# A transformer block on one core: output products of attention at a stretch, and row loads, normalization, row maxima and differences at other places

## The chip, the cores and the metric

The kernel runs on one core of a Trainium2 chip. The metric is the time of one execution on the device, in microseconds (us). The engines are TensorE (PE, with its weight loads as PEld), VectorE (DVE), ScalarE (ACT), GpSimd (POOL), and SyncE (SP), which here only issues DMAs. Each engine carries out its own list of instructions in the order of the program, and waits where one of them needs something from another engine or from a DMA.

## The reference

The input is 2048 rows of 512 numbers. The block is an attention with a memory between four segments of 512 rows, and a feed-forward part; all numbers are fp32.

```
mod = silu(c) @ w_mod                       # six rows: sa, ca, ga, sb, cb, gb
h = layernorm(x) * (1 + ca) + sa
x = x + ga * attention(h)                   # 32 heads of 16
h = layernorm(x) * (1 + cb) + sb
x = x + gb * (gelu(h @ w1 + b1) @ w2 + b2)  # 1792 inner columns

# attention, for each of four segments s of 512 rows and each head
p = softmax(qs @ ks.T / 4 + causal mask)
o = g * (phi(qs) @ M) / (phi(qs) @ z) + (1 - g) * (p @ vs)
M = M + phi(ks).T @ vs;  z = z + sum(phi(ks))
# then o @ wo
```

## The kernel before

There are three stages: projections (until about 190 us), attention (about 190 to 475 us), and the feed-forward part. Between the last two lies what this text calls the joint.

**Attention** takes the heads four at a time within a segment: 32 such groups, Q = 0 to 31, each of two pairs of heads, P = 2Q and 2Q + 1. For each pair, scores are made twice. `s_part` makes them with queries on the partitions, for the row maxima (L606, maxima on DVE at L613); parts 0 to 3 are query blocks with 512, 384, 256 and 128 keys. `st_part` makes them transposed, with the maxima already subtracted through three more rows of `qst` (L693); ACT takes the exponential (L708, L719) and POOL sets what lies above the diagonal to zero (L696, `causal`). `pv_part` multiplies with the values (L733). Both kinds of scores take the six PSUM banks `att` in turn.

For a pair of heads the smaller score blocks (256 and 128 keys) share a bank. For these there are two ways to the maxima: a third product adds the mask (L645) and one reduction on DVE takes both maxima (L617), or each head has a masked maximum of its own (L613). `PRM["m"]` and `PRM["mq"]` choose.

The maxima of a group go back into `qst` in three steps: `m_rows` splits them on POOL (L661), `m_put` turns them on PE (L667) with a copy on ACT, and `m_send` is a small DMA into `qst` (L675), issued by SP for the first groups and by ACT for the later ones (`PRM["msa"]`). Until it has landed, the group's transposed scores can't begin.

**The order** is written out by hand. One loop (L1013) runs over Q; this text calls one pass "loop Q". Its string `ORDER` names the score parts (S and T, with the part's number; the first mention in a pass is for pair 2Q, the second for 2Q + 1; S runs four pairs ahead) and twenty slots c0 to c19 between them:

```
ORDER = ('S1 c0 T2 T3 T2 c1 S2 c2 S3 T3 S3 c3 c4 c5 T5 S0 c6 c7 T0 c8 c9 '
         'T1 T4 S2 c10 c11 T5 S1 c12 T4 S0 c13 T0 c14 T1 c15 c16 c17 c18 c19')
```

Everything else has a position, 20 times the loop plus the slot; `ap(position, f, ...)` puts it there. So 466 is slot c6 of loop 23. Some positions that do not change: `m_rows` of group Q at 20Q - 26, `m_put` at 20Q - 17 (slot c3 of loop Q - 1), `load_stacks` (two DMAs of 384 KB) at c15, `pv_part` at c11 and c16 to c18.

**Two groups make a unit U.** The sums go to memory and come back packed (`pv_store`, `pv_in`); the reciprocals of the denominators are stored and spread (`den`, `den_store`, `rb_in`); `mix` joins them with the memory's part; `o_hi` and `o_lo` split the result for three products. For segments 0 to 2, `wo_part` multiplies with `wo` (L821, three products of 512 columns in the bank `mm`): for each of four row blocks four parts, at positions 240 + 160s + `PRM["wo"][s]`, then `wo_out` adds the input rows (DVE at L839, POOL at L837) and `wo_store` writes the rows to memory. These are then read back by `ln2_load` (positions `in`), their statistics are taken (`stat`, `rstd`), and `ln2_apply` normalizes them (`on`; L568, on POOL for segment 0 and on DVE for segment 1). `ln2_turn` transposes them on PE (L574; positions `ht` 502, 509, 516, 523 for segment 0).

**The joint** begins at L1161: what is left of the last units, the third segment's output products (`wo_seg`, `wo_late`), and the first operands of the feed-forward part, which uses a scheme with seven products for each 2 x 2 blocks. `r_sub` makes differences of operands on DVE (L886), `r_hi` and `r_lo` split them.

**The feed-forward part** runs over quads n = 0 to 13 (L1113), each with steps 0 to 6; `bg(n, i, f, ...)` puts background work at step i of quad n, where i over 6 runs on into the next quad. The rows of segments 2 and 3 are loaded, normalized and turned there.

## Time and profile before

| | us |
|---|---|
| three executions | 785.7, 789.17, 786.71 |
| median | 786.71 |
| the profiled execution | 789.61 |
| its span | 787.9 |

The span is that of the engines' instructions within the profiled execution. Busy times and waits below come from this one execution. In the views, a row of the timeline or the chain begins with the start and the length in us, then the engine, the line of the kernel and what is written and read; "x3" is the number of instructions merged into the row; brackets tell how long the engine stood idle before it and what ended that. A row of the waits tells who waited, for whom, the total in us, how often, and the longest. A row of stretches gives for each engine the busy time with the number of instructions, then the granted clock of TensorE, the busy share of the DMA engines and GB/s. Ends of matmuls are modelled: matmuls overlap, and the start of the next one tells more than the end.

### The profile page before, as it was taken

How to read it: one execution, taken by the hardware profiler on the slowest of the kernel's cores; microseconds unless marked ns; L12 is line 12 of the kernel's file. 1: busy time of each engine (PE TensorE's matmuls, PEld its weight loads, DVE VectorE, ACT ScalarE, POOL GpSimd, SP SyncE). 2: the span in 40 equal slices, each digit the busy share in tenths (PEclk: the TensorE clock that was granted, in tenths of full speed). 3: DMA queues.
4: the chain of work that ended last, by engine and by line, in shares of the span. 5: the costliest groups of instructions: out<-in, count | busy, mean ns of one | idle time of the engine just before them, and what ended most of it. 6: DMA issues, size and time to landing. Idle time of an engine off the chain costs nothing.

```text
span 787.9 us, 14128 instructions
## 1 busy us (share of the span) xinstructions
PE 767.7 (97%) x4577; PEld 532.6 (68%) x4577; DVE 553.6 (70%) x1456; ACT 472.6 (60%) x910; POOL 315.4 (40%) x535
## 2 busy tenths in 40 slices
PE   8999999999999999998999998999999999999998
PEld 4887776877554445554445446887888888888887
DVE  5686687548988788887977898867669764432423
ACT  3565546474888877776778676666645346652221
POOL 1357367261568556655696661133000404200000
PEclk9999999999999999999999999999999999999999
DMA  9596857497465566768677854595565624445543
GB/s 337 183 313 230 296 179 231 147 297 244 130 199 158 165 203 194 214 197 231 189 178 205 238 155 146 186 311 189 194 235 195 204 96 161 161 148 172 171 127 116
DMA packets 108818, 156.10 MB, mean 198 GB/s; under 512 B 16324, under 2 KB 55620, under 8 KB 108744
## 3 DMA queue, kind: packets, MB, share of 16 engines
q1 hardware_dynamic: 106758, 153.36, 62.1%
q10 hardware_dynamic: 1986, 1.84, 0.7%
q8 instruction: 36, 0.59, 0.3%
q14 instruction: 38, 0.31, 0.1%
HBM read 93.95 MB, written 60.83 MB: 196 GB/s over the span
## 4 chain that ended last, share of the span: by engine, by line
PE 74%; DMA 7%; DVE 7%; POOL 5%; issue 3%; ACT 3%; ACTq 0%; SPq 0%; DVEq 0%; POOLq 0%
PE att L693 7%; PE pv L733 7%; PE bx L1080 7%; PE att L606 6%; PE q L313 6%; PE bx L1346 5%; PE by L1346 5%; PE bv L1346 5%; PE k L313 4%; PE bv L1080 3%; PE v L464 3%; PE spare L1346 2%; PE mm L821 2%; DMA qst<-ms 2%; PE mm L1346 2%
## 5 line engine op out<-in xcount | busy, mean ns | idle before, releaser
L613 DVE CUSTOM_DVE_ANT_0 dump<-att,maskb 128x384 bf16<-128x384 f32 (+3 forms) x400 | 188.3, 524 | 38.8 <-PE att L606 22.1
L708 ACT ACTIVATE pt<-att 128x384 f32<-128x384 f32 (+1 forms) x256 | 125.5, 545 | 17.1 <-PE att L693 13.1
L696 POOL TENSOR_SCALAR_AFFINE_SELECT pt<-pt 128x256 f32<-128x256 f32 x256 | 104.1, 419 | 72.9 <-ACT pt L708 44.2
L693 PE MATMUL att<-qst,kst 99*128 99x256 bf16 (+3 forms) x512 | 108.0, 301 | 6.0 <-DMA qst<-ms 5.4
L606 PE MATMUL att<-kst,qst 96*128 96x384 bf16 (+3 forms) x400 | 94.0, 317 | 0.3 <-DVE nm L613 0.2
L693 PEld LDWEIGHTS <-kst 99*128 99x128 bf16 x512 | 44.1, 98 | 73.7 <-issue 36.2
L719 ACT ACTIVATE pt<-att 128x256 f32<-128x256 f32 (+1 forms) x128 | 62.3, 494 | 33.0 <-PE att L693 19.8
L865 POOL TENSOR_TENSOR wb<-wa 128x256 f32<-128x256 f32 x24 | 20.3, 845 | 151.8 <-DMA wa<-in_w 149.1
L733 PE MATMUL pv<-pt,V 128*32 128x512 f32 (+1 forms) x992 | 79.8, 439 | 0.0
L136 DVE TENSOR_TENSOR gl<-s,gh 128x512 fp32r<-128x512 f32 x34 | 24.1, 708 | 42.2 <-ACT gh L133 42.2
L733 PEld LDWEIGHTS pv<-pt,V 128*32 128x32 f32 x992 | 25.8, 109 | 35.9 <-issue 30.6
L133 ACT ACTIVATE gh<-s 128x512 fp32r<-128x512 f32 x34 | 21.3, 628 | 46.8 <-PE spare L1346 17.1
L606 PEld LDWEIGHTS <-qst 96*128 96x128 bf16 x400 | 32.9, 99 | 17.7 <-issue 12.4
L1085 ACT ACTIVATE s<-s,b1t 128x512 f32<-128x512 f32 x42 | 30.3, 722 | 21.9 <-DVE s L1089 21.8
L1089 DVE TENSOR_TENSOR s<-bv,s 128x512 f32<-128x512 f32 x28 | 19.3, 690 | 31.4 <-PE bv L1080 21.3
L613 DVE DVE_READ_ACCUMULATOR2_ANT nm<- 128x1 f32 x400 | 33.3, 83 | 0.0
L617 DVE TENSOR_REDUCE nm<-att 128x2 f32<-128x512 f32 (+1 forms) x56 | 28.7, 553 | 3.8 <-PE att L645 3.8
L509 POOL TENSOR_TENSOR q<-qr,q 128x512 bf16<-128x512 f32 x16 | 18.7, 1167 | 26.8 <-ACT q L508 26.5
L500 POOL TENSOR_SCALAR qp<-qp 128x512 f32<-128x512 f32 x12 | 19.2, 1603 | 24.6 <-ACT qp L495 24.6
L136 DVE TENSOR_TENSOR w1ml<-s,w1mh 128x512 fp32r<-128x512 f32 x18 | 13.0, 722 | 21.7 <-ACT w1mh L133 21.7
L661 POOL TENSOR_TENSOR nm<-nm 128x16 f32<-128x16 f32 x64 | 13.9, 218 | 33.7 <-DVE nm L613 31.0
L133 ACT ACTIVATE w1mh<-s 128x512 fp32r<-128x512 f32 x18 | 11.3, 628 | 26.3 <-PE spare L1346 11.6
(362 smaller groups left out, 2090.0 us busy)
## 6 DMA issues: line engine op xcount, KB each, us to landing
GD<-s SPq DMA_DIRECT2D x56, 256.0 KB
s<-GD SPq DMA_DIRECT2D x52, 256.0 KB
kst<-KD SPq DMA_DIRECT2D x32, 384.0 KB
qst<-QD SPq DMA_DIRECT2D x32, 384.0 KB
TD<-ts SPq DMA_DIRECT2D x32, 256.0 KB
xt<-X2D SPq DMA_DIRECT2D x28, 256.0 KB
wa<-in_w SPq DMA_DIRECT2D x28, 256.0 KB
QD<-q SPq DMA_DIRECT2D x16, 384.0 KB
```

Source lines behind the costliest of these rows:

```text
L133: act.activation(hi, src, AF.Copy)
L136: lo_eng.tensor_tensor(out=lo, in0=src, in1=hi.bitcast(F32), op=ALU.subtract)
L313: pe.matmul(ps, a[:, k, 128 * g:128 * g + 128], b[k], start=(k == 0 and i == 0), stop=(k == KB - 1 and i == 2))
L606: pe.matmul(ps, q_of(P, h, i), k_of(P, h, 128 * (i + 1)), start=True, stop=True)
L613: v.tensor_tensor_reduce(out=dump[n_dump[0] % 2][:, :n], in0=src, in1=maskb[:, 512 - n:], scale=-1.0, scalar=-4 * NEG, op0=ALU.add, op1=AL ...
L693: pe.matmul(ps, k[:99, e, 128 * j:128 * j + 128], q[:99, e, 128 * j:512], start=True, stop=True)
L696: pool.affine_select(out=t, in_=t, pattern=pattern, compare_op=ALU.is_ge, fill=0.0, base=0, channel_multiplier=-1)
L708: act.activation(pt[:, h, :], ps[:, :n], AF.Exp, scale=0.25)
L719: act.activation(pt, pv_, AF.Exp, scale=0.25)
L733: pe.matmul(ps[32 * c:32 * c + 32, lo:hi], V[4 * s + j][:, VW * hd:VW * hd + 32], pt[:, c % 2, lo - o:hi - o], start=start, stop=stop)
L1080: pe.matmul(ps, a[:, i, k, :], b[k], start=start and k == 0 and c == 0, stop=k == 1 and c == 2, skip_group_check=not start)
L1346: pe.matmul(ps, a[:, c], w[:, lo:hi], start=(f == 0 and i == 0), stop=(last and i == 2))
```

## The change

- The output products of segments 0 and 1 move from the slots c2 and c5 to c3 and c4, which follow each other without scores between them; in segment 2 the four parts at c2, c5, c8 and c14 move to c3, c3, c4, c4. `wo_x`, `wo_out` and `wo_store` move with them.
- `m_send` comes one slot after `m_put` instead of two, and SP issues it for groups under 13 instead of 10.
- For groups under 14 the blocks of 256 keys take masked maxima instead of a mask product and a reduction.
- The row loads and the normalization of segments 0 and 1 have other positions.
- In the joint, the subtraction `t2` comes ahead of a weight split, and `t3` and `t4` come in quad 0 behind `o_hi` and `o_lo` of unit 14.
- The rows of segment 3 are loaded in four steps instead of one, and the turns of segments 2 and 3 come two steps later.

```diff
- 'msl': 2,
- 'msa': 10,
+ 'msl': 1,
+ 'msa': 13,
...
- 'wo': [[20 * i + o for i in range(8) for o in (2, 5)]] * 2 + [[20 * i + o for i in range(4) for o in (2, 5, 8, 14)]],
+ 'wo': [[20 * i + o for i in range(8) for o in (3, 4)]] * 2 + [[20 * i + o for i in range(4) for o in (3, 3, 4, 4)]],
...
- 'ln': [{'in': [388, 397, 408, 417], 'stat': [418, 425, 437, 445], 'rstd': 449, 'on': [460, 467, 481, 487]},
-        {'in': [528, 537, 548, 568], 'stat': [565, 577, 585, 597], 'rstd': 603, 'on': [624, 626, 628, 630]}],
+ 'ln': [{'in': [327, 367, 387, 407], 'stat': [418, 425, 437, 445], 'rstd': 449, 'on': [455, 475, 479, 495]},
+        {'in': [527, 530, 547, 567], 'stat': [565, 577, 585, 597], 'rstd': 603, 'on': [624, 626, 628, 630]}],
...
- 'm': [1, 1, 1, 1],
+ 'm': [[0, 1, 0, 1], [1, 1, 1, 1]],
...
-                if PRM["m"][2 * p + i] and Q >= PRM["mq"]:
+                if PRM["m"][Q >= PRM["mq"]][2 * p + i]:
...
         r_hi(0, "t1")
+        r_sub(0, "t2")
         w_lo(0, 0)
-        r_sub(0, "t2")
         w_hi(0, 1)
...
         rest(14, "mix")
-        for n in ("t3", "t4"):
-            r_sub(0, n)
...
-        for n, i, f, *a in ((0, 0, rest, 14, "o_hi", "o_lo"), (0, 1, w_hi, 0, 2), (0, 1, w_hi, 0, 3),
+        for n, i, f, *a in ((0, 0, rest, 14, "o_hi", "o_lo"), (0, 0, r_sub, 0, "t3"), (0, 0, r_sub, 0, "t4"), (0, 1, w_hi, 0, 2), (0, 1, w_hi, 0, 3),
...
-        bg(3, 2, ln2_load3)
+        for b, i in enumerate((2, 3, 5, 6)):
+            bg(3, i, ln2_load3, b)
...
-                bg(n, 12 + d, ln2_turn, s, d, (mm, spare)[d % 2])
+                bg(n, 14 + d, ln2_turn, s, d, (mm, spare)[d % 2])
```

More of the change, by code (lines that the diff above doesn't have):

```diff
@@ L1223, in block_kernel, with ln2_load3 @@
             bg(n, i, f, *a)
-        def ln2_load3():
-            ln2_load(3, None, [gx[0](f"x3_{b}", F32) for b in range(4)])
+        x3 = []
+        def ln2_load3(b):
+            if b == 0:
+                x3.extend(gx[0](f"x3_{i}", F32) for i in range(4))
+            ln2_load(3, b, x3)
         def ln2_applies(s, lo, hi):
```

## The prediction

> **What bounds the kernel now.** I read first the page, then who TensorE (PE) waited for, then the chain of work in order of time, then timelines of single stretches.

> ```profile
> span 787.9 us, 14128 instructions
> ...
> PE 767.7 (97%) x4577; PEld 532.6 (68%) x4577; DVE 553.6 (70%) x1456; ACT 472.6 (60%) x910; POOL 315.4 (40%) x535
> ```

> PE is busy 97% of the span, so a change pays only where it shortens PE's own work or one of its few waits. These are the waits that matter (us in total, times, longest):

> ```profile
> PE att L693 <- DMA qst<-ms: 5.4, 5, 2.9
> PE bv L821 <- DVE ol L810: 2.8, 1, 2.8
> PE att L643 <- ACT pt L719: 2.0, 3, 1.1
> ...
> PE pv L667 <- POOL nm L661: 1.6, 2, 1.2
> ...
> PE mm L574 <- DVE xt L568: 0.5, 1, 0.5
> PE mm L574 <- ACT hr L576: 0.4, 1, 0.4
> ```

> The chain of waits gives the loop times; the eight matmuls of `pv` come once a loop:

> ```profile
> 237.00 0.99 PE pv L733 x8
> ...
> 244.70 1.00 PE pv L733 x8
> ...
> 328.59 1.00 PE pv L733 x8
> ...
> 337.14 0.99 PE pv L733 x8
> ...
> 354.24 0.99 PE pv L733 x8
> ...
> 361.15 9.02 DMA qst<-ms
> ...
> 376.04 0.99 PE pv L733 x8
> ```

> An early loop takes 7.70 us, one with output products 8.55, and the two from 354.24 to 376.04 take 21.80, that is 4.70 more than 2 x 8.55. The chain there lies on the send of the maxima of Q=21, which needed 9.02 us. PE idled 2.9 of it; the rest is the clock:

> ```profile
> 360.00:380.00 20.00, 17.07 (x133) 8.43 (x132) 15.59 (x68) 11.83 (x26) 10.08 (x21) 0.91 0.85 230
> ```

> A granted clock of 0.91 over 20 us is 1.8 us lost: 2.9 + 1.8 = 4.7. [...]

> **Sends.** `msl` moves the send one slot, past nothing on its own queue: nothing. `msa` moves Q=10 to 12 from ACT to SP:

> ```profile
> 266.88 1.36 ACTq L675 DMA_DIRECT2D qst<-ms  x1
> ```

> ACT's queue stands still while it issues, and the exponentials behind it hold the banks PE wants: the 2.0 us of L643 above, 3 times, these three. On SP the sends of Q below 10 cost PE nothing visible. But Q=11 is sent just behind the load of `gab`, and may land late: I take -1.5 (between -2.2 and 0).

> **Row maxima.** For Q under 14 the 256-wide pair loses its mask product, and gets two masked maxima for one reduction (28 times).

> ```profile
> 242.04 0.27 PE L645 MATMUL att<-maskb,identb 128*128 128x256 bf16 x1
> 242.16 0.22 PE L643 MATMUL att<-kst,qst 96*128 96x128 bf16 x1
> ...
> 242.27 0.27 PE L645 MATMUL att<-maskb,identb 128*128 128x256 bf16 x1
> 242.56 0.32 PE L693 MATMUL att<-qst,kst 99*128 99x384 bf16 x1
> ```

> ```profile
> L613 DVE CUSTOM_DVE_ANT_0 dump<-att,maskb 128x256 bf16<-128x256 f32 x72 | 27.5, 420 | 3.8 <-ACT pt L708 3.1 <-issue 0.7
> ...
> L617 DVE TENSOR_REDUCE nm<-att 128x2 f32<-128x512 f32 x28 | 19.3, 690 | 2.9 <-PE att L645 2.9
> ```

> A mask product costs PE 0.12 (242.04 to 242.16), so 28 are 3.4 us at most. But L693 at 242.56 started 0.29 after the product ahead of it, which itself takes 0.12: PE was already waiting there for a bank, so of a loop's two removed products the first only lengthens that wait. DVE pays 2 x 27.5/72 - 19.3/28 = 0.07 us each. With one product saved and some 0.05 given back in a loop, twelve loops make -0.8 (between -3.4 and +2).

> **Output products.** Two parts of three products stood at c2 and c5, now at c3 and c4, behind `m_put`. The same place in loop 20:

> ```profile
> 358.24 0.50 PE L606 MATMUL att<-kst,qst 96*128 96x384 bf16 x2
> ...
> 359.20 0.48 PE L821 MATMUL mm<-woh,oh 128*128 128x512 f32 x1
> ...
> 359.99 0.29 PE L606 MATMUL att<-kst,qst 96*128 96x128 bf16 x2
> 360.11 0.33 PE L693 MATMUL att<-qst,kst 99*128 99x384 bf16 x1
> ```

> ```profile
> 359.19 0.55 DVE L613 CUSTOM_DVE_ANT_0 dump<-att,maskb 128x384 bf16<-128x384 f32 x1
> ```

> `att` has six banks. The L693 at 360.11 takes over the bank whose second 384-wide maximum ended at 359.19 + 0.55 = 359.74. Today the part at 359.20 to 359.99 covers that. Without it PE gets there at about 359.40 and can go on at 359.80: 0.40 us of new waiting. What is then covered instead, PE's next work behind the pair, had no wait to lose (8.55 is dense). Does a joined stretch save anything?

> ```profile
> 580.00:600.00 20.00, 20.00 (x90) 16.57 (x89) 16.34 (x28) 10.18 (x19) 0.00 (x0) 1.00 0.65 227
> ```

> In dense work a product takes 20/90 = 0.222, three 0.67; the stretch above takes 0.79, of which 0.11 is the tail of the pair ahead. I take 0.02 saved for each joint, 0.12 as the other bound (28 joints: 3.4 us). Net +0.38 a loop; in the loops 12 to 21, 26 and 27 that is +4.6 (between -3 and +6). [...]

> **Row loads.** SP around the late send:

> ```profile
> 356.16 0.45 SPq L556 DMA_DIRECT2D xt<-X2D  x1
> ...
> 361.01 0.34 SPq L556 DMA_DIRECT2D xt<-X2D  x1
> ```

> Two loads of 256 KB stand in the burst ahead of the send. The new places take one to loop 18 and the other ahead of `rb_in`, for whose data SP waits before it. At the 230 GB/s of the window row 512 KB are 2.2 us, and `m_put` comes 0.3 earlier in its loop: of 2.9 us idle 0.4 is left, and no half clock: -4.3 (between -4.7 and 0, as the new loads in loops 16 and 18 stand ahead of sends too). The other sends that land late (28, 29, 31) gain the 0.3: -0.5 together.

> **Normalization.** POOL works without a break from loop 22 on:

> ```profile
> 384.58 1.28 POOL L793 TENSOR_TENSOR opk<-opk,rbB 128x512 f32<-128x512 f32 x1
> ...
> 406.67 2.07 POOL L568 TENSOR_SCALAR xt<-xt,cmv,crs 128x512 f32<-128x512 f32 x1
> 408.70 1.48 POOL L696 TENSOR_SCALAR_AFFINE_SELECT pt<-pt 128x256 f32<-128x256 f32 x4
> 410.15 0.51 POOL L661 TENSOR_TENSOR nm<-nm 128x16 f32<-128x16 f32 x2
> ```

> ```profile
> 409.35 0.60 PE L574 MATMUL att<-ident,xt 128*128 128x128 f32 x4
> ...
> 411.54 0.29 PE L693 MATMUL att<-qst,kst 99*128 99x128 bf16 x2
> ```

> Each application costs POOL 2.07 us. Behind `m_rows` they no longer delay it, which ends the 1.6 us of L667. But the last application, at 495, now follows four selects, `m_rows` and a select: it ends not at 406.67 + 2.07 = 408.74 but after 1.45 (408.70 to 410.15) for the four, 0.46 for `m_rows`, 0.37 (a quarter of 1.48) for the select, and the 0.4 by which loop 22's joined parts hold up POOL's first selects: 411.4. The first turn (position 502, unmoved) needs it. PE, today there at 409.35, would come without the part ahead of it (0.79) and the wait for `m_rows` (1.2), but with 3 x 0.38 more in the loops before: 408.5. A new wait of about 2.9 us, L574 behind POOL. After it come the turn (0.4), the scores and `m_put` (0.5) and six products (1.4 to 1.5), and the next L693 stands at 413.8 where it stood at 411.54: +2.3 for the loops 22 to 25 (between -2 and +4, the latter with the half clock again).

> **The joint and after.** `o_lo` of unit 14 stood behind four subtractions:

> ```profile
> 490.43 1.76 DVE L810 TENSOR_TENSOR ol<-opk,oh 128x512 fp32r<-128x512 f32 x1
> ...
> 497.78 0.69 DVE L810 TENSOR_TENSOR ol<-opk,oh 128x512 fp32r<-128x512 f32 x1
> ```

> ```profile
> 498.95 0.39 PE L821 MATMUL bv<-woh,oh 128*128 128x512 f32 x1
> ```

> Ahead of them it removes most of PE's 2.8 us. But unit 15's `o_lo`, at the end of a chain of DMAs that nothing here shortens, ends at 498.47, and PE's second product needs it at 499.2 today. What is gained beyond 0.7 is lost there again: -0.7 (between -2.8 and +0.5). The turns of the later rows, two steps later, lose their 0.5 + 0.4 us: -0.9 (between -0.9 and +0.5). The loads of the last rows in four issues stand beside dense products: nothing.

> **Sum.** -1.5 - 0.8 + 4.6 - 4.3 - 0.5 + 2.3 - 0.7 - 0.9 = -1.8 us against the profiled execution's 789.6 (span 787.9): 787.8. That execution is 2.9 above the median of 786.7, so 784.9.

> **Rivals.** (1) Normalization lands in time and the bank wait shrinks into others. If POOL is not behind at the turn, loops 22 to 25 give -0.1 rather than +2.3; if the wait at c3 is not paid, 4.6 go. Both: -8.8, 777.9; one: 780 to 782.5. For it: the selects wait for ACT too, and POOL has more time in longer loops. Against it: POOL's rows without a gap. [...] (3) Slower: an idle time of 2.9 us halves the clock, as it did behind Q=21. It decides at two places, the turn of loop 25 (2.9 us by my sum) and the send of Q=21, if the burst is late for other reasons than the two loads. Price: 1.8 at the first, 4.3 not gained at the second: +4.3, 791.0. For it: the window row; against it: the two loads are the only thing in that burst that the loops before lack. (4) The moves do nothing since SP and POOL run behind anyway: 786.7; the lists are executed in order, so hardly.

> **Numbers.** Forecast 0.45, rival 1 0.25, rival 2 0.06, rival 3 0.21, rival 4 0.03. 0.5% is 3.9 us, about what a measurement of this kernel can tell from no change. The forecast's own range, 781 to 789, is nearly all within it (0.07 below); rivals 1 and 2 lie below but for a tenth, rival 3 above. Faster 0.36, same 0.41, slower 0.23. The range reaches to rival 1 and to rival 3: 777 to 791.5.

> **What would show it.** L643's wait on ACT gone; a wait of about 0.4 at L693 behind DVE's maxima in each loop from 12; no clock below 1.00 at 360 to 380; L667 without POOL, and one L574 in `att` waiting 3 us for POOL; L821's wait on `ol` moved from unit 14 to 15. It is wrong if the loops from 12 still take 8.55 or less, if the turn does not wait, or if a send lands late elsewhere.

## The result, and the profile after

| | before | after |
|---|---|---|
| median of four executions each, us | 787.24 | 797.44 |
| span of the profiled execution, us | 787.9 | 796.5 |
| that execution's time, us | 789.61 | 798.23 |

The changed kernel is slower by 1.3%: ratio 1.0127, 95% interval 1.0103 to 1.0150. The prediction said 784.9, between 777.0 and 791.5.

The page of the changed kernel shows PE as busy as before, 97%, although a mask product has gone from 28 places. Matmuls that run at half clock are counted as busy, too: in a row of e5 in the last section PE is busy 3.41 us of 3.41 at a granted clock of 0.50.

```profile
span 796.5 us, 14174 instructions
...
PE 773.8 (97%) x4549; PEld 535.8 (67%) x4549; DVE 554.6 (70%) x1540; ACT 473.2 (59%) x910; POOL 315.3 (40%) x535
```

The starts of `m_put` (L667) cut both profiled executions into the same stretches:

| stretch | before | after | difference |
|---|---|---|---|
| start to Q=0 | 191.95 | 190.50 | -1.45 |
| Q=0 to 10 | 74.29 | 73.79 | -0.50 |
| Q=10 to 13 | 25.73 | 24.12 | -1.61 |
| Q=13 to 21 | 68.42 | 71.47 | +3.05 |
| Q=21 to 25 | 40.25 | 36.73 | -3.52 |
| Q=25 to 27 | 19.80 | 24.83 | +5.03 |
| Q=27 to 31 | 37.75 | 39.98 | +2.23 |
| Q=31 to the end | 329.76 | 335.09 | +5.33 |

The first stretch says nothing: in the 18 profiles of this text it takes 190.0 to 192.9 us. From Q=0 to Q=25 the changed kernel gains 2.6 us net, although it loses 3.05 in the plain loops (Q=13 to 21). The two loops behind Q=25 and everything from Q=27 on then lose 12.6. Whom PE waits for in the changed kernel (total, times, longest):

```profile
PE att L574 <- DVE xt L568: 4.0, 3, 1.9
PE att L693 <- DVE nm L613: 3.6, 17, 0.3
PE att L574 <- POOL xt L568: 2.5, 1, 2.5
...
PE att L693 <- DMA qst<-ms: 1.6, 3, 1.3
PE bx L1080 <- DVE rt3l L899: 1.1, 1, 1.1
...
PE mm L574 <- ACT hr L576: 0.7, 1, 0.7
PE bv L821 <- DVE ol L810: 0.6, 1, 0.6
```

The second row is the wait at c3 that was predicted, the third is the turn of loop 25, predicted at 2.9. The first was not predicted. In the chain of waits, plain loops now lie 8.93 apart, not 8.55:

```profile
327.25 1.00 PE pv L733 x8
...
336.18 1.00 PE pv L733 x8
```

PE's timeline shows the three places themselves:

```profile
359.61 0.32 PE L693 MATMUL att<-qst,kst 99*128 99x384 bf16 x1 [0.20 <-DVE nm L613]
...
407.88 0.47 PE L574 MATMUL att<-ident,xt 128*128 128x128 f32 x1 [2.52 <-POOL xt L568]
...
478.03 0.30 PE L574 MATMUL att<-ident,xt 128*128 128x128 f32 x1 [1.93 <-DVE xt L568]
479.00 0.47 PE L574 MATMUL att<-ident,xt 128*128 128x128 f32 x1 [0.66 <-DVE xt L568]
480.85 3.49 PE L574 MATMUL att<-ident,xt 128*128 128x128 f32 x14 [1.38 <-DVE xt L568]
```

The turn at 407.88 stands behind the last application on POOL, which ends at 405.76 + 2.07 = 407.83:

```profile
403.42 1.51 POOL L696 TENSOR_SCALAR_AFFINE_SELECT pt<-pt 128x256 f32<-128x256 f32 x4
404.90 0.50 POOL L661 TENSOR_TENSOR nm<-nm 128x16 f32<-128x16 f32 x2
405.36 0.41 POOL L696 TENSOR_SCALAR_AFFINE_SELECT pt<-pt 128x256 f32<-128x256 f32 x1
405.76 2.07 POOL L568 TENSOR_SCALAR xt<-xt,cmv,crs 128x512 f32<-128x512 f32 x1
```

The stretches of 20 us say what became of the clock (the third figure from the end):

```profile
360.00:380.00 20.00, 19.17 (x149) 10.03 (x148) 18.19 (x84) 14.14 (x31) 11.27 (x25) 1.00 0.71 211
400.00:420.00 20.00, 17.48 (x128) 9.26 (x121) 11.22 (x47) 12.20 (x25) 12.50 (x24) 0.83 0.56 170
...
480.00:500.00 20.00, 19.15 (x102) 14.35 (x103) 14.22 (x23) 11.12 (x19) 3.03 (x2) 0.86 0.42 126
```

The lost clock at 360 to 380 has gone. But half clock goes with each of the two longer idle times: 0.17 of 20 us is 3.4 us lost at the turn of loop 25, that is 6.8 us at half. The lost clock at 480 to 500 lies in the turns of segment 1, which is why their last row takes 3.49 us for 14.

Why those rows come late is seen on DVE. Its rows before and after the first casts of `rb11h` (`r_hi` of `early`), in the changed kernel:

```profile
461.62 0.24 DVE L776 TENSOR_SCALAR dn<-dn,omg 128x32 f32<-128x32 f32 x1
464.55 0.69 DVE L839 TENSOR_TENSOR xb<-mm,xb 128x512 f32<-128x512 f32 x1 [2.68 <-PE mm L821]
465.16 2.02 DVE L129 CAST rb11h<-hr 128x512 fp32r<-128x512 f32 x2
...
480.25 1.00 DVE L568 TENSOR_SCALAR xt<-xt,cmv,crs 128x512 f32<-128x512 f32 x2
```

and in the kernel before:

```profile
458.07 0.76 DVE L129 CAST rb11h<-hr 128x512 fp32r<-128x512 f32 x2
...
472.60 1.31 DVE L568 TENSOR_SCALAR xt<-xt,cmv,crs 128x512 f32<-128x512 f32 x2
```

Before, the casts began as `m_put` of Q=31 did (458.19). Now they begin 3.7 us behind it (461.42), behind `wo_out` at L839, which waits 2.68 us for PE's output products. The operands of the casts had long been there: ACT wrote the last of them before 424. From the casts on, DVE works nearly without a break until the rows of segment 1 are normalized, so whatever is lost ahead of the casts arrives at the turns.

### The profile page after: what moved, and what is told of

Read it like the earlier page. It is cut to its first block, busy times and chain, and to the rows that moved or that the text cites. A ratio compares the mean times of both kernels' runs of the same rounds, so it can differ in the third digit from the quotient of the medians.

```text
span 796.5 us, 14174 instructions
## 1 busy us (share of the span) xinstructions
PE 773.8 (97%) x4549; PEld 535.8 (67%) x4549; DVE 554.6 (70%) x1540; ACT 473.2 (59%) x910; POOL 315.3 (40%) x535
## 4 chain that ended last, share of the span: by engine, by line
PE 77%; DVE 7%; POOL 5%; DMA 4%; issue 4%; ACT 3%; ACTq 0%; DVEq 0%; POOLq 0%
PE bx L1080 9%; PE att L693 6%; PE pv L733 6%; PE q L313 6%; PE att L606 6%; PE bx L1349 5%; PE by L1349 5%; PE bv L1349 5%; PE bv L1080 5%; PE k L313 4%; PE mm L821 3%; PE v L464 3%; PE spare L1349 2%; PE by L1080 2%; PE mm L1349 2%
## 5 line engine op out<-in xcount | busy, mean ns | idle before, releaser
L613 DVE CUSTOM_DVE_ANT_0 dump<-att,maskb 128x384 bf16<-128x384 f32 (+1 forms) x456 | 206.9, 511 | 37.0 <-PE att L606 22.6
L696 POOL TENSOR_SCALAR_AFFINE_SELECT pt<-pt 128x256 f32<-128x256 f32 x256 | 104.8, 420 | 75.3 <-ACT pt L708 41.2
L708 ACT ACTIVATE pt<-att 128x384 f32<-128x384 f32 (+1 forms) x256 | 124.4, 544 | 14.5 <-PE att L693 10.5
L693 PE MATMUL att<-qst,kst 99*128 99x256 bf16 (+3 forms) x512 | 106.4, 301 | 6.3 <-DVE nm L613 3.6
L606 PE MATMUL att<-kst,qst 96*128 96x384 bf16 (+1 forms) x456 | 102.6, 311 | 1.8 <-DVE nm L613 0.8
L693 PEld LDWEIGHTS <-kst 99*128 99x128 bf16 x512 | 44.5, 98 | 68.5 <-issue 35.0
L719 ACT ACTIVATE pt<-att 128x256 f32<-128x256 f32 (+1 forms) x128 | 62.5, 491 | 35.8 <-PE att L693 34.2
L733 PE MATMUL pv<-pt,V 128*32 128x512 f32 (+1 forms) x992 | 79.8, 439 | 0.0
L606 PEld LDWEIGHTS <-qst 96*128 96x128 bf16 x456 | 39.5, 98 | 24.9 <-issue 16.2
L733 PEld LDWEIGHTS pv<-pt,V 128*32 128x32 f32 x992 | 25.8, 109 | 36.7 <-issue 31.2
L1089 DVE TENSOR_TENSOR s<-bv,s 128x512 f32<-128x512 f32 x28 | 19.3, 689 | 32.8 <-PE bv L1080 23.0
L613 DVE DVE_READ_ACCUMULATOR2_ANT nm<- 128x1 f32 x456 | 38.0, 83 | 0.0
L500 POOL TENSOR_SCALAR qp<-qp 128x512 f32<-128x512 f32 x12 | 18.8, 1562 | 26.2 <-ACT qp L495 26.2
L661 POOL TENSOR_TENSOR nm<-nm 128x16 f32<-128x16 f32 x64 | 13.9, 217 | 34.3 <-DVE nm L613 31.5
L313 PE MATMUL q<-Ahh,wqh 128*128 128x512 f32 x64 | 26.1, 407 | 0.0
```

Source lines behind the costliest of these rows:

```text
L313: pe.matmul(ps, a[:, k, 128 * g:128 * g + 128], b[k], start=(k == 0 and i == 0), stop=(k == KB - 1 and i == 2))
L606: pe.matmul(ps, q_of(P, h, i), k_of(P, h, 128 * (i + 1)), start=True, stop=True)
L613: v.tensor_tensor_reduce(out=dump[n_dump[0] % 2][:, :n], in0=src, in1=maskb[:, 512 - n:], scale=-1.0, scalar=-4 * NEG, op0=ALU.add, op1=AL ...
L693: pe.matmul(ps, k[:99, e, 128 * j:128 * j + 128], q[:99, e, 128 * j:512], start=True, stop=True)
L696: pool.affine_select(out=t, in_=t, pattern=pattern, compare_op=ALU.is_ge, fill=0.0, base=0, channel_multiplier=-1)
L708: act.activation(pt[:, h, :], ps[:, :n], AF.Exp, scale=0.25)
```

## The experiments

The medians are of executions taken beside executions of the kernel before on the same chip. "Clock" counts the executions whose granted clock was 1.00 over the whole execution.

| run | median, us | ratio to the kernel before | clock 1.00 |
|---|---|---|---|
| changed kernel | 797.44 | 1.0127 [1.0103, 1.0150] | 0 of 4 |
| e1_wo_back | 787.24 | 1.0011 [0.9991, 1.0032] | 4 of 12 |
| e2_wo2_back | 791.02 | 1.0068 [1.0045, 1.0091] | 3 of 12 |
| e3_on_back | 795.88 | 1.0115 [1.0087, 1.0144] | 0 of 6 |
| e4_early | 796.08 | 1.0109 [1.0076, 1.0141] | 1 of 6 |
| e5_rest | 786.08 | 0.9995 [0.9974, 1.0016] | 8 of 12 |
| e6_rest_in | 784.14 | 0.9963 [0.9942, 0.9984] | 8 of 12 |
| e7_out_late | 792.54 | 1.0069 [1.0049, 1.0089] | 0 of 6 |
| e8_c2c2 | 790.60 | 1.0060 [1.0039, 1.0081] | 6 of 11 |
| e9_in_back | 784.93 | 0.9983 [0.9963, 1.0003] | 8 of 12 |
| e11_gate | 783.02 | 0.9951 [0.9933, 0.9969] | 12 of 12 |
| e12_sends_back | 783.87 | 0.9977 [0.9958, 0.9997] | 9 of 12 |
| e13_before_msl | 786.50 | 1.0007 [0.9985, 1.0029] | 2 of 12 |

**Which part costs.** All output products back (e1), or only those of segment 2 (e2):

```diff
-'wo': [... (3, 4)]] * 2 + [... (3, 3, 4, 4)]]
+'wo': [... (2, 5)]] * 2 + [... (2, 5, 8, 14)]]   # e1
+'wo': [... (3, 4)]] * 2 + [... (2, 5, 8, 14)]]   # e2
```

> The changed kernel with all output products back at c2 and c5 (segment 2: c2, c5, c8, c14); the rest of the change stays. Theory D (the products cost 0.38 us in each of the loops 12 to 27, and in segment 2 they also put wo_out ahead of early work in DVE's queue, which ends the attention some 4 us late and halves the clock once more): about 3 us back in the loops 13 to 21, 2 in the loops 22 to 27, 5 at the end of attention and in the joint: 786 to 788, that is 0 to -1.5 us against the kernel before. The wait of L574 for DVE's L568 at position 644 falls from 4.0 to under 1 us. Rival N (normalization of segment 0 and the half clock behind it carry most of the loss): the products give back only the 5 us of the loops, 792, and the wait at 644 stays.

> The changed kernel with only segment 2's output products back at c2, c5, c8, c14. Theory D: the loops to 27 keep their loss, the end of attention and the joint get back some 5 us: 792 to 793, that is +5 us against the kernel before; L839 no longer waits 2.7 us for PE ahead of the casts of rb11h, and L574 waits for L568 under 1 us in place of 4.0. Rival J (the end is late for the order of differences in the joint or for the late sends): within 1 us of the changed kernel, 797.

Both came out as theory D said, but for e2 being 1 us faster than its 792 to 793. By the medians, segment 2's products cost 797.4 - 791.0 = 6.4 us, those of segments 0 and 1 791.0 - 787.2 = 3.8. By the ratios, which set each run against executions beside it, it is 4.6 and 4.5 us. In e2's waits of PE, L574 behind DVE has gone and the wait at c3 is still there:

```profile
PE att L693 <- DVE nm L613: 3.4, 16, 0.3
```

In e1 it is down to one:

```profile
PE att L693 <- DVE nm L613: 0.3, 1, 0.3
```

**Which part of segment 2's move.** In e7 the products stay where the change put them; only `wo_out` and `wo_store` go back to c15:

```diff
-ap(w[3] + 1, own, "mm", (s, b), wo_out, (s, b), True)
+ap(w[3] + (11 if s == 2 else 1), own, "mm", (s, b), wo_out, (s, b), True)
...
-    ap(w[3] + 1 + PRM["xol"], wo_store, s, b)
+    ap(w[3] + (11 if s == 2 else 1) + PRM["xol"], wo_store, s, b)
```

> The changed kernel, its products as changed, but segment 2's wo_out and wo_store stay at c15, where they were before. Theory D (not the place of segment 2's products costs the end of attention, but wo_out, which went with them to c5 and holds DVE's queue): the waits of L839 for PE of 1.8 and 2.7 us go, L574 at 644 waits under 1 us, the end of attention comes 4 to 5 us earlier: 792 to 793, +5 to +6 against the kernel before, as with the products themselves moved back. Rival B (the joined products themselves are the cost: bank waits and covers lost in loops 28 to 31): 796 to 797.

792.5: theory D. By the medians, 4.9 of the 6.4 us are `wo_out` alone; by the ratios e7 gives back as much as e2, 4.6 us. So `wo_out` carries most of the loss, and what segment 2's products cost by themselves is not shown. The profiles agree: from `m_put` of Q=31 to the first product of the feed-forward part they have 31.4 us in the changed kernel, 26.3 in e7 and 24.9 in e2. On DVE the casts now begin at 459.29, 0.76 behind `m_put` of Q=31 (458.53), and nothing waits ahead of them:

```profile
459.14 0.24 DVE L776 TENSOR_SCALAR dn<-dn,omg 128x32 f32<-128x32 f32 x1
459.29 0.96 DVE L129 CAST rb11h<-hr 128x512 fp32r<-128x512 f32 x2
```

In e4 the same queue is changed at the other end: the early casts go ahead of `wo_out`.

```diff
-'early': [605, 615]
+'early': [600, 610]
```

> The changed kernel with the early casts and differences of b11 and b21 at 600 and 610 instead of 605 and 615, so that DVE has them ahead of wo_out in its queue. Theory D (DVE's in-order queue stands still behind wo_out while work that is ready waits): the 2.7 us of L839 waiting for PE are filled with 2 to 4 us of work, L574 at 644 waits 1 to 2 us in place of 4.0, 793 to 795, that is +6 to +8 against the kernel before. Rival J (DVE is late for other reasons, or the order in the joint decides): 797, with L574 waiting 4.0 us as before.

The median, 796.1, doesn't tell this run from the changed kernel and misses the 793 to 795 of theory D. Its profiled execution, the fastest of six (792.1), has L574 waiting 1.9 us for L568 in place of 4.0, as theory D said. So the mechanism is there, and the gain of the wait alone is 2 us.

**Normalization.** In e3 segment 0's applications go back:

```diff
-'on': [455, 475, 479, 495]
+'on': [460, 467, 481, 487]
```

> The changed kernel with segment 0's normalization back at 460, 467, 481, 487. Theory D, with the normalization as a part of its own: the wait of L574 behind POOL in loop 25 (2.5 us) and the half clock behind it (6.8 us long, 3.4 lost) go, some 1.5 us of L667 waiting for POOL come back: 4 to 5 us gained, 793, that is +6 against the kernel before; the end of attention is unchanged, with its 4.0 us of L574 behind L568. Rival (the half clock at the end stems from the one in loop 25): the end gains too, 789 to 790.

The turn's wait and the half clock behind it have gone from the profile, and 1.5 us of L667 behind POOL are back. The stretch from Q=25 to 27 takes 20.17 us instead of 24.83. The end of attention is unchanged (4.1 us of L574 behind L568), so the half clock there is not an echo of the first. But the median, 795.9 where 793 was expected, shows only 1.6 of the 4.7 us, and the intervals overlap. With the products back, the same edit is worth 787.2 - 786.1 = 1.2 (e1 to e5), again with overlapping intervals. What the wait costs thus depends on how often the half clock follows it. The second profile of the changed kernel (time 796.54) shows this:

> The changed kernel, unchanged, a second profile. Theory D: 8.93 in each of the loops 14 to 20, L574 waits 2 to 2.6 us for POOL in loop 25, and at 644 about 4 us for L568, in this execution too; how often the half clock follows may differ by a stretch of 3.4 us. Rival: one of the two waits is absent, and the time is then 3 us or more below 797.4.

```profile
PE att L574 <- DVE xt L568: 4.1, 3, 1.9
PE att L693 <- DMA qst<-ms: 4.0, 3, 1.4
...
PE att L574 <- POOL xt L568: 1.3, 1, 1.3
```

The wait at 644 recurs in full. In loop 25 a late send held PE first, so POOL was less late, 1.3 us where 2 to 2.6 was expected, and no half clock followed there.

**What is left of the change.** In e5 products and normalization are both back (the edits of e1 and e3).

> The changed kernel with the output products and segment 0's normalization where they were before; row loads, row maxima, sends, the joint and the turns of later rows stay changed. Theory D (products and normalization are the whole loss, the rest is a gain): the ledger of the run with the products back (-3.0 for the loops 0 to 12, +1.9 for a late send behind the row load at 327, -4.2 for the loops 21 to 24, +0.3 for 25 and 26, -0.8 in the joint) gives -5 to -6 against the kernel before: 781 to 782. Rival C (the single profile flatters, and the gains before loop 24 are taken back by the next late send): -1 to 0, 786.

786.1: rival C. Theory D's ledger was read off one profile and was wrong by 5 us. What the other parts gain in the median is 0.7 us of the 8.7 that the prediction gave them, and the interval includes nothing. For e9 the row loads go back as well:

```diff
-'in': [327, 367, 387, 407]
+'in': [388, 397, 408, 417]
...
-'in': [527, 530, 547, 567]
+'in': [528, 537, 548, 568]
```

> As the run that has products and normalization back, with the row loads of segments 0 and 1 back too (388, 397, 408, 417 and 528, 537, 548, 568): only sends, row maxima, the joint and the turns of later rows stay changed. Theory S (two row loads in the burst ahead of the send of Q=21 cost 3 us of idle time and with the half clock 4.3): the send of Q=21 takes 8 to 9 us, m_put of Q=21 to 23 takes 20 to 22 us in place of 17.9, but the 1.0 at Q=18 goes: 787 to 788, 1 to 2 us worse than that run. Rival P (the stall in the profile of the kernel before was peculiar to that execution): within 0.5 us of that run or better, no half clock at 370.

784.9: rival P. No gain from the change's row loads is to be seen. In e5, with a load at 327, the send of Q=17 is late (9.52 us from Q=17 to 18, 8.55 in e9); but it is late in e11 below as well (9.62), whose loads stand elsewhere, so the load is not shown to be the cause. And the send of Q=21, with the loads back in front of it, is nearly in time (L693 waits 0.3 us). In the chain of waits of e9 it stands with 6.42 us, where the execution of the prediction had 9.02:

```profile
358.74 6.42 DMA qst<-ms
```

So was the stall of Q=21 that the prediction priced at 4.7 us a fact of the kernel before? Three more profiles of it (e10, e14, e15), unchanged:

> The kernel before, unchanged, for a second profile. Theory S: the send of Q=21 again lands 2 to 3 us late, m_put of Q=21 to 23 takes 21 to 22 us, with a stretch of half clock at 370 to 376. Rival P: 17 to 19 us there and no half clock.

> The kernel before, unchanged, a third profile. Theory V (the profile on which the prediction's sum was made lies above the median since this execution had the late send and the half clock in full; others have less of it): where the time is under 787.5, m_put of Q=21 to 23 takes under 20 us or no clock under 1.00 is seen. Rival (the difference from run to run lies in the stages before attention or in the feed-forward part): the loops take 20.7 to 21.8 there whatever the time is.

The text for e15 is the same. Their rows for 360 to 380, in this order:

```profile
360.00:380.00 20.00, 18.16 (x141) 9.17 (x140) 16.66 (x70) 12.73 (x29) 10.57 (x23) 0.91 0.77 227
```

```profile
360.00:380.00 20.00, 18.57 (x154) 9.53 (x151) 17.61 (x76) 14.43 (x32) 11.44 (x26) 1.00 0.86 255
```

```profile
360.00:380.00 20.00, 18.72 (x154) 9.53 (x152) 18.21 (x84) 13.99 (x31) 11.25 (x25) 1.00 0.90 245
```

Times 790.28, 787.33 and 785.09; from Q=21 to 23 they take 20.7, 18.8 and 18.6 us, and the execution of the prediction took 21.8. Two dense loops are 17.1. So the send is late every time, by 1.3 to 2.9 us at L693, but half clock followed in two of four. The execution on which the sum was made had the longest stall of the four: theory V. In e13 the earlier send alone is put into the kernel before:

```diff
-'msl': 2
+'msl': 1
```

> The kernel before with one edit: the send comes one slot behind m_put instead of two. Theory M (the send of Q=21 is late because it is issued into the burst of SP's transfers that follows c15; 0.3 to 0.6 us earlier it is ahead of enough of it, whatever the row loads do): the send of Q=21 takes under 6.5 us, m_put of Q=21 to 23 takes 17.5 to 18.5 us in place of 20.7 to 21.8, no half clock at 370; in the median 1 to 2 us gained, 785. Rival S (only the two row loads make it late): 20.5 us or more there, 786.3.

Theory M falls: the two loops take 19.65, the send is still 2.3 us late there, and the time is the same. Rival S, with 20.5 or more, is not met either; 19.65 lies within the 18.6 to 21.8 of the kernel before. Neither the earlier send alone nor, in e12, the old send with other row loads shows what made it punctual in e9. With the loads in other loops (e12) it is punctual as well: Q=21 to 23 takes 17.8. Why e9 differs from e13 stays open; the send's landing differs by over 1 us among executions of one kernel (1.3 to 2.9 us of waiting at L693 in the four above), and each version has one profile.

**A version that beats both.** Sends of odd Q have little time to spare: in the kernel before, those of Q=13 to 25 landed 1.5 us or less ahead of their use, or late. Those of even Q, 12 to 26, landed 2.7 to 5.0 us ahead. (The program sends the traffic of a unit at the time of the odd ones; that this is the reason was not tested.) e6 is e5 with the row loads in odd loops, ahead of even Q; e11 moves the load of `gab`, too; e12 is e6 with the sends as they were.

```diff
-'in': [327, 367, 387, 407]
+'in': [307, 347, 387, 427]   # e6, e11, e12
...
-'gate': 197
+'gate': 217   # e11
...
-'msl': 1, 'msa': 13
+'msl': 2, 'msa': 10   # e12
```

> As the run before, with segment 0's row loads at 307, 347, 387, 427, all in odd loops. Theory S (a row load matters where it shares the DMA engines with a late send; sends of odd Q, issued in even loops, take 5 to 7 us and those of even Q under 3.5): the 1.1 us of L693 waiting for the send of Q=17 and the 0.7 at Q=21 go, 1.5 to 2 us better than the run before. Rival (the sends of odd Q are late by the traffic of their unit alone): within 0.5 us of it.

> As the run with row loads at 307, 347, 387, 427, with the load of gab at 217 (loop 10) instead of 197 (loop 9), so that it stands ahead of the send of Q=12, not of Q=11. Theory S (sends of even Q have 3 to 4 us to spare, those of odd Q none): the loop from Q=11 to 12 takes 7.6 in place of 8.5 us, 783.3, 0.9 better than that run. Rival: the next late send takes it back, 784.1.

> As the run with row loads at 307, 347, 387, 427, with the sends as before (two slots behind m_put, Q=10 to 12 from ACT). The prediction gave the sends 1.5 us: the three waits of L643 or L606 on ACT's L719, 2.0 us in all, come back: 785 to 786. Rival (the wait on ACT only moves to the late send of Q=11): 784.

e6 is 2 us better than e5, as expected, and Q=17 to 18 takes 8.55 again, but the intervals overlap. e11 is the best version: 783.0, ratio 0.9951, so 3.3 us faster than the kernel before (its median there 786.29). Its loop from Q=11 to 12 takes 7.63 in place of 8.51, as expected; the next late send, at Q=17, takes 1.1 back. That it is better than e6 isn't shown. What stands out is that no execution of it had a stretch of half clock: the mean granted clock is 1.000 in all 12. e12 shows no value for the sends: 783.9 against 784.1. The waits on ACT that the prediction counted are back, now 1.9 us at L606, and the late send of Q=11 has gone.

**A joined stretch.** e8 is e5 with both parts of segments 0 and 1 at c2:

```diff
-'wo': [20 * i + o for i in range(8) for o in (2, 5)]
+'wo': [20 * i + o for i in range(8) for o in (2, 2)]
```

> As the first run of this call, with the products of segments 0 and 1 joined at c2 (both parts there) instead of c2 and c5. Theory D (the price of the change's place is the cover that the part at c2 gives to the maxima ahead of L693; a joined stretch by itself saves 0.02 a loop or so): the loops 14 to 20 take 8.53 to 8.56 us, the whole is within 1 us of the first run. Rival W (joining saves the open part of a weight load, 0.1 a stretch): 8.43 to 8.45 a loop, 1.6 us better.

Neither expectation holds: plain loops take 9.19 us, 0.64 more than with c2 and c5, and the run is 4.5 us slower than e5. PE's waits in e8 name the cause:

```profile
PE att L606 <- ACT pt L719: 8.3, 14, 1.2
```

With c5 empty, PE reaches the next score part before ACT has freed its bank. So each place had its own cover: the part at c2 hides DVE's maxima (0.38), the one at c5 ACT's exponentials (0.64). The loop is dense because the two are apart.

## Why the prediction was wrong

By the medians, products of segments 0 and 1 cost 3.8 us, those of segment 2 with `wo_out` 6.4, normalization 1.2, and the rest gained 0.7: +10.7, and +10.2 was measured. The prediction had +4.6, nothing, +2.3 and -8.7.

**Output products, +4.6: right.** 3.8 in the medians, and 3.05 from Q=13 to 21, where eight times 0.38 is 3.04. PE's open idle time is only 0.2 a loop (3.6 us in 17 waits); the rest shows as wider spacing of the matmuls around it (in the timeline after, the L693 behind the wait starts 0.75 us after the first of the four products of L606 ahead of it, 358.86 to 359.61; in the prediction's timeline the same two pairs take 0.14 and 0.12). The prediction's bound of 0.12 gained for each joint is not supported: no loop was shorter for it. Rival 2 of the chances, a larger gain from joining the products, was not met either. A weight load of L821 takes 0.19 us in the trace before (median), and no run shows a part of it that joining saves: plain loops took 8.55 us with the products apart, 8.93 and, in e8, 9.19 with them joined.

**The failed step: segment 2.** The part "Output products" priced the loops 12 to 21, 26 and 27, and gave segment 2 and `wo_out`, which moves with the products, no price beyond 0.02 us saved at each joint. `wo_out` went from c15 to c5, in loop 30 just ahead of the first early cast (both at 605), and stands in DVE's queue before it. The order of DVE's list was there to be read, and so was DVE's work, nearly without a break, from the casts at 458.07 to the last application at 472.60 in the trace before; the prediction followed who waits on PE and looked at POOL and SP, but not at what queues on DVE behind the instruction that moved. This is worth 6.4 us by the medians and 4.6 by the ratios, most of it `wo_out`. In the trace after, DVE stood idle for 2.68 us at `wo_out`, ahead of a cast whose operands had long been there.

**The second failed step: the gains of the rest, -8.7.** They came out as 0.7 in the median. By terms:

- Row loads, -4.3: the stall is real, but was 4.7 us only in the execution profiled. The prediction summed against that execution and then subtracted its distance from the median (2.9) from the result, as if that distance had been spread over everything. A good part of it was the stall itself. And the row loads were not what ended it: e9 has them in their old places and a stall of only 0.3 us at L693. The rival that the moves do nothing (4) was nearest here.
- Sends, -1.5: the waits of L643 went, and Q=11's late send came (L693 idle 1.3 us), as the prediction's bound of 0 allowed; e12 shows nothing.
- Row maxima, -0.8: about right, 0.08 a loop and 0.5 up to Q=10.
- Late sends, -0.5: not seen. The loops 27 to 30 took 2.2 us more, 0.4 of it the price at c3 in loop 27, the last with segment 1's products.
- The joint, -0.7, and the turns of later rows, -0.9: the wait for `o_lo` of unit 14 went from 2.8 to 0.6, as predicted, but the subtractions it used to stand behind now come later, and PE waits 1.1 us for `rt3l` (L1080). The turns still wait for `hr`, 0.7 us. In e5, e6, e9 and e11 Q=31 to the first product of the feed-forward part takes 24.4 to 24.5 us, in the four profiles of the kernel before 24.4 to 25.4. Together perhaps 0.5. What one profile could not show: in three of the four profiles of the kernel before (e10, e14, e15), and in e13, half clock followed the wait for `o_lo`, and cost 1.7 us more. Only the execution of the prediction was spared that (see the last section), so the term leaves out part of what this wait costs. What its removal is worth in the median was not measured by itself.

**Normalization, +2.3: right in mechanism.** L574 waited 2.5 us behind POOL where 2.9 was forecast, L667's wait went. From Q=22 to 26 that gave +1.3. The half clock came with it, as rival 3 had it: 2.8 more in the next loop, where its price was 1.8.

**The range.** Rival 3 was the right kind of loss. It happened at two places, the second of which, the turns of segment 1, the prediction did not have.

## What to carry to other kernels

- A moved step takes its followers along. For each one, list what stands behind it in its own engine's queue; here an instruction that waited 2.68 us there held up casts that were ready, and the turns at the end of attention waited 4.0 us.
- A product put between two waits is a cover; before joining two of them, ask what each covers. Here the covers were 0.38 and 0.64 us a loop, and joining saved nothing.
- A stall seen in one profile is a draw from a spread (here 1.3 to 2.9 us, with half clock behind it in two profiles of four). Take a second profile, or the spread of the times, before pricing its removal, and do not subtract the distance from the median again.

## What the hardware showed

In the profile before the granted clock is 0.50 from 371.55 to 374.96, that is for 3.41 us; in the profile after for 6.83 us each from 407.26 to 414.09 and from 478.94 to 485.77, and the 64.85 between these two are 19 times 3.41. So both profiles were cut into pieces of 3.41 us, counted from these changes of the clock, and the time that PE idles in a piece was taken, all gaps together. Ahead of the three stretches at half clock PE idled 2.09 us of a piece in the profile before, and 1.89 and 2.54 in the profile after; in no other piece at full clock, as long as PE had work left, more than 1.58 and 1.30. (Ends of matmuls are modelled, so the hundredths are not certain.) In the first pieces at half clock PE idled 0.62 and 1.43 us in the profile after, and a second such piece followed; it idled in none of the piece in the profile before, and full clock followed. No run set the idle time by itself, so what decides was not tested.

The length of a gap alone did not tell what followed. The wait for `o_lo` of unit 14 was 2.82 us long in the kernel before. The pieces cut it at 491.01 into 1.59 and 1.23, and the clock stayed at 1.00. The first row is PE's, the others are the pieces, with PE's busy time first and the clock third from the end:

```profile
492.24 0.50 PE L821 MATMUL bv<-woh,ol 128*128 128x512 f32 x1 [2.82 <-DVE ol L810]
```

```profile
487.60:491.01 3.41, 1.83 (x8) 1.15 (x7) 3.41 (x6) 2.87 (x7) 1.06 (x1) 1.00 0.11 37
491.01:494.42 3.41, 2.18 (x10) 1.80 (x10) 3.41 (x5) 1.46 (x3) 0.63 (x1) 1.00 0.69 216
494.42:497.84 3.42, 3.42 (x17) 2.83 (x16) 3.31 (x8) 1.12 (x2) 0.00 (x0) 1.00 0.90 297
```

In e14, the same kernel, the same wait was shorter, 2.56 us. It lay within the 3.41 us ahead of a stretch at half clock:

```profile
490.17 0.50 PE L821 MATMUL bv<-woh,ol 128*128 128x512 f32 x1 [2.56 <-DVE ol L810]
```

```profile
487.39:490.80 3.41, 0.85 (x4) 0.54 (x4) 3.41 (x5) 3.19 (x6) 1.45 (x1) 1.00 0.35 112
490.80:494.22 3.42, 3.42 (x10) 2.64 (x9) 3.32 (x7) 0.00 (x0) 0.00 (x0) 0.50 0.82 285
```

Two more runs have nearly the same idle time in 3.41 us, and differ in what followed. In e5 two gaps of 1.46 and 0.22 us, in a row with 1.67 idle, were followed by half clock:

```profile
486.62 0.50 PE L821 MATMUL bv<-woh,oh 128*128 128x512 f32 x1 [1.46 <-ACT oh L127]
487.35 0.50 PE L821 MATMUL bv<-woh,ol 128*128 128x512 f32 x1 [0.22 <-DVE ol L810]
```

```profile
485.18:488.59 3.41, 1.74 (x6) 1.24 (x7) 2.68 (x3) 1.73 (x4) 1.81 (x1) 1.00 0.16 48
488.59:492.00 3.41, 3.41 (x9) 2.30 (x7) 3.41 (x7) 2.79 (x5) 0.00 (x0) 0.50 0.91 279
```

In e4 a gap of 2.03 us was not. The row from 407.49 has 1.65 us of idle time:

```profile
409.14 0.33 PE L574 MATMUL att<-ident,xt 128*128 128x128 f32 x1 [2.03 <-POOL xt L568]
```

```profile
407.49:410.90 3.41, 1.76 (x12) 1.51 (x13) 1.18 (x10) 1.35 (x4) 3.38 (x4) 1.00 0.63 186
410.90:414.32 3.42, 3.42 (x27) 1.63 (x27) 2.65 (x9) 2.53 (x5) 0.98 (x3) 1.00 0.47 108
```

**The same cast takes different times.** The two casts of `rb11h` take 0.42 us each in the kernel before (0.76 for both in the row above), and 0.60 and 1.50 in the changed one (2.02 for both). POOL was working on `amB` at the time:

```profile
465.45 1.44 POOL L800 TENSOR_TENSOR amB<-amB,rm 128x512 f32<-128x512 f32 x1
```

The other casts point the same way. Of the eight casts of `rb11h` and `rb21h` in the traces before and after, only the one of 1.50 us coincides with 1.2 us of this instruction; the others take 0.41 to 0.62. Those of `rb11h` take 0.42 in e2, and 0.42 and 0.63 in e7. That POOL's work is the cause was not tested by moving it. The late casts thus met another delay of about 1.2 us.
